# Splitting the first gate-weight load into small pieces on two queues, with the early products reordered to match

## The chip, the cores and the metric

The kernel runs on one core of one Trainium2 chip. The metric is the device time of one execution in microseconds. Executions of the kernel before repeat closely on a quiet chip: three runs gave 179.41 to 180.25 us, median 179.52 us. The traces also give a "span", which is about 1.8 us shorter than the time of the same execution (177.6 us of 179.39 us).

Engines are named as in the profile: PE is TensorE (matrix products), PEld its weight loads, ACT is ScalarE, DVE is VectorE, POOL is GpSimd, SP is SyncE (it issues most DMAs). PSUM is the memory that PE writes its products to, and from which ACT and DVE copy them. In the traces here each engine works through its own instructions in the order in which the program lists them, ready or not.

## The reference, cut to what matters

```python
def reference(A_x, A_w_r, A_w_i, B_x, B_w_gate, B_w_up, B_w_down):
    x = A_x                                       # 1 x 2048 x 512, bf16
    xn = _layernorm(x, axis=-1)
    # A: rfft2 of xn, times (w_r + i w_i), irfft2
    # B: (gelu(xn @ w_gate) * (xn @ w_up)) @ w_down,   512 -> 1792 -> 512
    return x + _A_ref(xn, A_w_r, A_w_i) + _B_ref(xn, B_w_gate, B_w_up, B_w_down)
```

Everything starts from xn, and the first products of B need three things: a normalised and transposed tile of x (128 rows), the gate weights, and the up weights.

## The kernel before

The 2048 rows are 16 tiles of 128. A weight "slice" is 128 columns of the 1792; `e` runs over the four blocks of 128 along the inner dimension of 512. The kernel does not write its instructions in a fixed order. It lists operations with assumed durations, dependencies and priorities, and a small scheduler (`_Plan`), which runs when the kernel is built, simulates them and fixes each engine's order from that. What the planner believes about a DMA's landing is this:

```python
if o.nbytes:                                   # a DMA
    wire = max(wire, o.end + 1.0) + o.nbytes / 0.34e6
    o.end = wire + 1.0                         # its landing, as the plan sees it
```

The loads of the opening, in order of issue:

```python
load_x(0, 1)                                   # x tile 0, 128 KB
d_ident = load_ct("ident", "ident", "ACT")
load_x(1, 1)
load_w(0, 2, ("SP", "ACT"))                    # gate and up slices 0-1, 256 KB each
# ... activation table load on ACT ...
load_x(2, 2)                                   # x tiles 2-3, 256 KB
load_w(2, 4)
load_w(4, 6)
load_x(4, 4)
load_w(6, 10)
load_x(8, 4)
load_w(10, 14)
```

Layernorm of the first four tiles, on DVE but for one small step on POOL, and the transposes. Tile 0 is handled in two halves, which share one PSUM tile:

```python
def pe_transpose(c, due):
    b = _Buf("S")
    n = len(XN[c])
    for h in range(n):
        # ...
        def mm(h=h, es=es):
            if h == 0:
                psum(f"tp.{c}", [P, NE, P], BF16)          # one tile for both halves
            for e in es:
                nc.tensor.transpose(tiles[f"tp.{c}"][:, e], xn[:, c, e * P:(e + 1) * P], ident)

        def ev(es=es, eng=(nc.scalar.copy, V.tensor_copy)[h]):   # half 0 copied by ACT, half 1 by DVE
            eng(out=xnT[c // 4][:, es[0]:es[-1] + 1, c % 4], in_=tiles[f"tp.{c}"][:, es[0]:es[-1] + 1])
        # ...

first = layernorm(0, 1, -28, (), 2)
layernorm(1, 1, -25, first)
for c in range(4):
    if c == 2:
        layernorm(2, 2, -22, XT[0])
    pe_transpose(c, -28 + 3 * c)
    if c < NGAP:
        dummies(GAP, -29.9 + 3 * c, XN[c], P)              # dummy products
```

The first products (`glu(first tile, tiles, first slice, slices)`), two slices at a time, gate then up:

```python
FIRST = [(0, 1, 0, 4), (1, 1, 0, 4), (0, 2, 4, 2), (2, 2, 0, 2), (2, 2, 2, 2), (2, 2, 4, 2)]
```

Of the kernel before, what the change touches and what calls it, by code (L numbers as in the profile page):

```python
# [10 lines left out]
P = 128  # L11
# [6 lines left out]
S = 2048  # L18
D = 512
# [109 lines left out]
class _Plan:  # L129
# [19 lines left out]
    def run(self):  # L149
# [11 lines left out]
        while left:  # L161
            nxt, moved = None, False
            for e, ops in waiting.items():
# [6 lines left out]
                for o in ops:  # L170
                    if any(d.end is None for d in o.deps):
                        continue
                    at = max([d.end + d.lag + self.HOP for d in o.deps if d.eng != "PE" or o.eng != "PE"] + [0.0])
                    if o.nbytes and o.eng != "POOL" and len(lanes) >= 8:
                        at = max(at, sorted(lanes)[-8])
                    if at > now + 1e-9:
                        nxt = at if nxt is None else min(nxt, at)
                        continue
                    held = [rings[b.tag][-self.bufs[b.tag]] for b in o.new if len(rings[b.tag]) >= self.bufs[b.tag]]
                    if any(b.free is None for b in held):  # L180
                        continue
                    at = max([b.free for b in held] + [0.0])
                    if at > now + 1e-9:
                        nxt = at if nxt is None else min(nxt, at)
                        continue
                    if best is None or (o.prio, o.n) < (best.prio, best.n):
                        best = o
# [31 lines left out]
def kernel(  # L219
# [44 lines left out]
    warm = pc.tile([P, D], BF16, name="warm")  # L264
    eps = pc.tile([P, 2], F32, name="eps")
    tiles = {}

# [45 lines left out]
    def load_x(c0, n, eng="SP", deps=()):  # L313
        q = nc.sync if eng == "SP" else nc.scalar
        o = load(n * P * D * 2, lambda: q.dma_start(out=x_t[:, c0:c0 + n], in_=x_v[:, c0:c0 + n]), deps, eng=eng)
        for c in range(c0, c0 + n):
            XD[c] = o

    def load_w(f0, f1, engs=("SP", "SP")):
        a, b = f0 * P, f1 * P  # L320
        os = []
        for t, v, e in ((Wg_sb, wg_v, engs[0]), (Wu_sb, wu_v, engs[1])):
            q = nc.sync if e == "SP" else nc.scalar
            os.append(load(NE * P * P * 2 * (f1 - f0),
                           lambda t=t, v=v, q=q: q.dma_start(out=t[:, :, a:b], in_=v[:, :, a:b]), eng=e))
        for f in range(f0, f1):
            WD[f] = os

    def load_ct(first, last, eng="SP", deps=(), **kw):
        a, b = ccols[first][0], sum(ccols[last])  # L330
        q = nc.sync if eng == "SP" else nc.scalar
        return load(P * 2 * (b - a), lambda: q.dma_start(out=CT[:, a:b], in_=cap[:, a:b]), deps, eng=eng, **kw)

    load_x(0, 1)
    d_ident = load_ct("ident", "ident", "ACT")
    load_x(1, 1)
    load_w(0, 2, ("SP", "ACT"))
    add("ACT", 1.3, lambda: nc.scalar.activation(out=eps[:, 1:2], in_=eps[:, 0:1], func=AF.Gelu_apprx_tanh),
        (o_eps,), -900)
    load_x(2, 2)  # L340
    load_w(2, 4)
    load_w(4, 6)
    load_x(4, 4)
    load_w(6, 10)
    load_x(8, 4)
    load_w(10, 14)

# [26 lines left out]
    wb = _Buf("S")  # L374
    NWARM, NGAP, GAP = 10, 1, 4

# [21 lines left out]
    def layernorm(c0, n, due, after=(), halves=1):  # L398
        k = slice(c0, c0 + n)
        ag = []  # L400
        for c in range(c0, c0 + n):
            s = dve(0.6, lambda c=c: stats(c), [XD[c]] + list(after), due - 3.0 + 0.01 * (c - c0))
            ag.append(dve(0.15, lambda c=c: V.bn_aggr(out=mv[:, c], in_=tiles["st", c][:]), (s,), due - 3.2, ))
        e = dve(0.07, lambda: V.tensor_scalar(  # L404
            out=ve[:, k], in0=mv[:, k, 1], scalar1=EPS, scalar2=None, op0=ALU.add), ag, due - 5)
        r = add("POOL", 0.55, lambda: nc.gpsimd.tensor_tensor(  # L406
            out=rstd[:, k], in0=ve[:, k], in1=half[:, k], op=ALU.pow), (e, o_mem[1]), due - 5, lag=0.1)
        for c in range(c0, c0 + n):
            XN[c] = []
            for h in range(halves):  # L410
                d = slice(h * D // halves, (h + 1) * D // halves)
                XN[c].append(dve(0.04 + 0.29 / halves, lambda c=c, d=d: V.tensor_scalar(  # L412
                    out=xn[:, c, d], in0=x_t[:, c, d], scalar1=mv[:, c, 0:1], scalar2=rstd[:, c:c + 1],
                    op0=ALU.subtract, op1=ALU.mult), (r,), due - 2.5))
        return ag

    def pe_transpose(c, due):
        XT[c] = []
        b = _Buf("S")
        n = len(XN[c])  # L420
        for h in range(n):
            es = range(h * NE // n, (h + 1) * NE // n)

            def mm(h=h, es=es):
                if h == 0:
                    psum(f"tp.{c}", [P, NE, P], BF16)
                for e in es:
                    nc.tensor.transpose(tiles[f"tp.{c}"][:, e], xn[:, c, e * P:(e + 1) * P], ident)

            def ev(es=es, eng=(nc.scalar.copy, V.tensor_copy)[h]):  # L430
                eng(out=xnT[c // 4][:, es[0]:es[-1] + 1, c % 4], in_=tiles[f"tp.{c}"][:, es[0]:es[-1] + 1])

            o = pe(0.24 / n, mm, (XN[c][h], d_ident), due - 2, new=(b,) if h == 0 else (), use=(b,))
            XT[c].append((act, dve)[h](0.1 + 0.35 / n, ev, (o,), due - 30, use=(b,)))
# [4 lines left out]

    first = layernorm(0, 1, -28, (), 2)  # L440
    layernorm(1, 1, -25, first)
    for c in range(4):
        if c == 2:
            layernorm(2, 2, -22, XT[0])
        pe_transpose(c, -28 + 3 * c)
        if c < NGAP:
            dummies(GAP, -29.9 + 3 * c, XN[c], P)
    for c0, n, due in ((4, 2, 14), (6, 2, 16), (8, 4, 24), (12, 4, 32)):
        layernorm(c0, n, due)
        for c in range(c0, c0 + n):  # L450
# [10 lines left out]
    for k in range(2):  # L461
        for c, s, a, n in ((2, 1, 0, 7 * KC), (0, 0, 0, KC), (1, 1, 7 * KC, KC)):
            d_tw.append(dma(P * n * 2, lambda k=k, c=c, s=s, a=a, n=n: gather(k, s, c, a, n),
                            [g_idx] + XN[11], 20, eng="POOL", issue=1.2))

# [20 lines left out]
    def glu(c0, n, f0, nf=1, extra=()):  # L486
# [10 lines left out]
        def mm(nm, W, tag, a, b):  # L497
            if a == 0:
                psum(f"{nm}.{key}", [P, D], tag=tag)
            for f in range(a, b):  # L500
                for e in range(NE):
                    nc.tensor.matmul(tiles[f"{nm}.{key}"][:, f * w:f * w + w], lhsT=W[:, e, (f0 + f) * P:(f0 + f + 1) * P],  # L502
                                     rhs=rhs(e), start=(f + e == 0), stop=(f == nf - 1 and e == NE - 1),
                                     skip_group_check=nf > 1)

        g = [o for c in range(c0, c0 + n) for o in XT[c]]
        step = min(nf, 2)
        us = []
        for a in range(0, nf, step):
            deps = g[-1:] if a else g  # L510
            new = [([], []), ([gb], [ub])][a == 0]
            g = [pe(step * dur, lambda a=a: mm("g_ps", Wg_sb, "G", a, a + step), deps + [WD[f0 + a][0]], t,
                    new=new[0], use=(gb,))]
            us = [pe(step * dur, lambda a=a: mm("u_ps", Wu_sb, "U", a, a + step), us + g + [WD[f0 + a][1]], t,
                     new=new[1], use=(ub,))]
# [20 lines left out]

    FIRST = [(0, 1, 0, 4), (1, 1, 0, 4), (0, 2, 4, 2), (2, 2, 0, 2), (2, 2, 2, 2), (2, 2, 4, 2)]
    for c, n, f, nf in FIRST + [(0, 4, f, 1) for f in range(6, NFC)]:
        glu(c, n, f, nf)
# [387 lines left out]
```

## Time and profile before

| | before |
|---|---|
| median of three executions | 179.52 us |
| span of the profiled one | 177.6 us |
| PE busy | 173.4 us, 98% of the span |
| first PE instruction | 1.34 us |
| PE products and transposes | 1,100 |

The first lines are from the page of the kernel before: its span, the busy time of each engine, PE's busy tenths in 40 slices of the span, and the chain of work that ended last, by engine and by line (only the engine line is kept).

```profile
span 177.6 us, 3041 instructions
...
PE 173.4 (98%) x1100; PEld 92.9 (52%) x1100; DVE 118.1 (66%) x266; ACT 87.4 (49%) x158; POOL 18.6 (10%) x33
...
PE   6999999999999999999999999999999999999993
...
PE 91%; ACT 3%; DVE 3%; issue 1%; POOL 0%; DVEq 0%; POOLq 0%
```

PE is full from end to end, so a change can win only where PE is not full: the first slices. To see how much that is, take the start times of the single PE instructions. Back to back, products start every 56 ns for 128 columns, 109 ns for 256 and 216 ns for 512. What a start-to-start step takes beyond that is *excess*. The span is then the first PE start (1.34 us) + the ideal time of all products (169.73 us) + excess (3.62 us) + the tail from the last PE start to the end (2.92 us) = 177.6 us. Of the 3.62 us, 2.28 lie before 5.6 us (mostly ten dummy products of 512 columns, of which most start every 427 ns instead of 216; the texts call that pace cold), 1.06 between 5.6 and 12.3 us, none up to 60 us, and 0.28 is one stall at 75.7 us.

This is the table of stretches of the kernel before. Its columns are start and end of the stretch and its length, then busy time and (instructions) of each engine, the granted clock, the DMA engines' busy share, and the GB/s they moved.

```profile
0.00:5.60 5.60, 4.26 (x10) 1.31 (x10) 1.99 (x6) 1.49 (x2) 2.11 (x9) 1.00 0.62 182
5.60:12.30 6.70, 6.66 (x93) 5.82 (x92) 4.10 (x14) 2.84 (x6) 1.27 (x2) 1.00 1.08 330
12.30:60.00 47.70, 47.70 (x317) 27.12 (x315) 40.89 (x91) 29.81 (x56) 15.21 (x22) 1.00 0.79 209
```

This is the timeline of the opening of the kernel before. The columns are start, duration, engine, line, operation, out<-in, and in brackets how long the engine was idle before and what released it.

```profile
5.78 0.65 PE L428 MATMUL tp<-CT,xn 128*128 128x128 bf16 x4
...
6.47 0.37 ACT L431 COPY xnT<-tp 128x256 bf16<-128x256 bf16 x1 [3.29 <-PE tp L428]
...
6.88 0.29 DVE L431 COPY xnT<-tp 128x256 bf16<-128x256 bf16 x1 [0.83 <-ACT xnT L431]
6.89 0.82 PE L502 MATMUL g_ps<-xnT,Wg_sb 128*128 128x128 bf16 x8
...
8.42 0.59 ACT L431 COPY xnT<-tp 128x512 bf16<-128x512 bf16 x1 [1.58 <-PE tp L428]
...
8.84 0.62 PE L502 MATMUL u_ps<-xnT,Wu_sb 128*128 128x128 bf16 x8
```

Read it so: ACT copies the first transposed half of tile 0 at 6.47. DVE's copy of the other half waits for ACT's, and PE's first real product starts at 6.89. Tile 1 is copied by ACT at 8.42 and is therefore ready at 9.01.

### The profile page before, as it was taken

Reading aid. Unit: us, or ns where it says so; the run is one execution under the profiler, and the core shown is the slowest. Engines: PE = TensorE matmul, PEld = TensorE weight load, DVE = VectorE, ACT = ScalarE, POOL = GpSimd, SP = SyncE. Lnnn points to the kernel's source line nnn. Section 1 sums busy time; section 2 is a strip of 40 time slices with the busy share of each in tenths; the row PEclk is TensorE's granted clock in tenths of the full one; section 3 lists DMA queues with packets and bytes.
Section 4 is the critical chain, followed back from the end, with each engine's and each line's share of the span. In section 5 each row is a group of like instructions: output and inputs, shape, how many; then the busy total and the mean of one; then the engine's idle time right before and its main releaser. Section 6 shows DMA issues by size and latency. Waiting matters only on the chain.

```text
span 177.6 us, 3041 instructions
## 1 busy us (share of the span) xinstructions
PE 173.4 (98%) x1100; PEld 92.9 (52%) x1100; DVE 118.1 (66%) x266; ACT 87.4 (49%) x158; POOL 18.6 (10%) x33
## 2 busy tenths in 40 slices
PE   6999999999999999999999999999999999999993
PEld 2598545545554544554555455554445444544463
DVE  1869999999537995889999885336442541632522
ACT  3162437456789737999998855453111211211100
POOL 3212138743200000000000000000000000000000
PEclk9999999999999999999999999999999999999999
DMA  5999487999297001302211121100222221322212
GB/s 144 311 355 359 86 270 84 223 296 193 52 347 255 2 0 29 93 2 59 61 48 37 37 59 37 27 0 0 84 68 66 83 89 59 92 80 69 74 45 59
DMA packets 23182, 19.24 MB, mean 108 GB/s; under 512 B 8512, under 2 KB 21824, under 8 KB 23168
## 3 DMA queue, kind: packets, MB, share of 16 engines
q1 hardware_dynamic: 22176, 17.57, 35.0%
q0 software_dynamic: 320, 1.19, 3.1%
q10 hardware_dynamic: 672, 0.30, 0.6%
q8 instruction: 8, 0.13, 0.3%
q14 instruction: 6, 0.05, 0.1%
HBM read 13.28 MB, written 2.10 MB: 87 GB/s over the span
## 4 chain that ended last, share of the span: by engine, by line
PE 91%; ACT 3%; DVE 3%; issue 1%; POOL 0%; DVEq 0%; POOLq 0%
PE u_ps L502 25%; PE g_ps L502 25%; PE warm L380 3%; ACT E L652 2%; PE yp L818 2%; PE bp L581 2%; PE gp L767 2%; PE yp__2078 L872 2%; PE yp__1994 L872 2%; PE yp__1967 L872 2%; PE yp__1936 L872 2%; PE yp__1909 L872 2%; PE yp__1820 L872 2%; PE yp__1793 L872 2%; PE yp__1762 L872 2%; PE yp__1735 L872 2%
## 5 line engine op out<-in xcount | busy, mean ns | idle before, releaser
L502 PE MATMUL g_ps<-xnT,Wg_sb 128*128 128x512 bf16 (+2 forms) x264 | 58.1, 347 | 0.0
L502 PE MATMUL u_ps<-xnT,Wu_sb 128*128 128x512 bf16 (+2 forms) x264 | 57.9, 347 | 0.0
L527 DVE TENSOR_TENSOR hT<-u_ps,ge 128x512 bf16<-128x512 f32 x56 | 38.4, 685 | 17.5 <-PE u_ps L502 14.4
L519 ACT ACTIVATE ge<-g_ps 128x512 bf16<-128x512 f32 x56 | 33.5, 598 | 30.5 <-PE g_ps L502 26.5
L502 PEld LDWEIGHTS <-Wu_sb 128*128 128x128 bf16 x264 | 24.3, 98 | 22.3 <-DMA Wu_sb<-in_B_w_up_dram 0.2
L502 PEld LDWEIGHTS <-Wg_sb 128*128 128x128 bf16 x264 | 24.3, 98 | 20.7 <-issue 0.2
L872 PEld LDWEIGHTS <-hT 128*128 128x128 bf16 x252 | 23.0, 98 | 21.9
L824 ACT CAST yf<-yp 128x512 bf16<-128x512 f32 x16 | 9.3, 586 | 37.6 <-PE yp L818 37.6
L652 ACT CAST E<-ep 64x512 bf16<-64x512 f32 x32 | 18.5, 579 | 1.1 <-PE ep L646 0.7
L396 DVE BATCH_NORM_STATS2 st<-x_t 128x6 f32<-128x512 bf16 x16 | 10.5, 676 | 4.8 <-DMA x_t<-in_A_x_dram 4.8
L629 ACT CAST ds<-dp 128x512 bf16<-128x512 f32 x16 | 8.8, 589 | 1.1 <-PE dp L624 1.0
L773 ACT CAST Gs<-gp 128x512 bf16<-128x512 f32 x16 | 8.6, 593 | 1.0 <-PE gp L767 1.0
L406 POOL TENSOR_TENSOR rstd<-ve,half 128x2 f32<-128x2 f32 (+2 forms) x7 | 6.6, 949 | 21.9 <-DVE ve L404 21.9
L585 ACT CAST Bs<-bp 128x512 bf16<-128x512 f32 x16 | 8.3, 603 | 0.5 <-PE bp L581 0.5
L818 PEld LDWEIGHTS <-Gs 128*128 128x128 bf16 x64 | 4.8, 98 | 3.5
L380 PE MATMUL warm<-warm 128*128 128x512 bf16 (+1 forms) x14 | 5.1, 539 | 1.3 <-POOL half L373 1.3
L412 DVE TENSOR_SCALAR xn<-x_t,mv,rstd 128x512 bf16<-128x512 bf16 (+1 forms) x17 | 6.1, 399 | 0.3 <-POOL rstd L406 0.3
L818 PE MATMUL yp<-CT,Gs 128*128 128x128 bf16 x64 | 6.0, 219 | 0.0
L683 DVE TENSOR_TENSOR m<-X,TW 128x1024 bf16<-128x1024 bf16 x8 | 5.5, 692 | 0.2
L624 PEld LDWEIGHTS <-Bs 128*128 128x128 bf16 x64 | 4.4, 98 | 2.4
L689 DVE TENSOR_TENSOR m<-X,TW 128x1024 bf16<-128x1024 bf16 x8 | 5.5, 684 | 0.0
L646 PE MATMUL ep<-ds,CT 128*128 128x512 bf16 x16 | 5.4, 379 | 0.0
(103 smaller groups left out, 169.0 us busy)
## 6 DMA issues: line engine op xcount, KB each, us to landing
y<-in_A_x_dram SPq DMA_DIRECT2D x16, 128.0 KB, 2.1
F<-F SPq DMA_DIRECT2D x32, 64.0 KB, 2.0
out_dram<-y SPq DMA_DIRECT2D x15, 128.0 KB, 1.7
Wd_sb<-in_B_w_down_dram SPq DMA_DIRECT2D x2, 896.0 KB, 8.3
x_t<-in_A_x_dram SPq DMA_DIRECT2D x3, 512.0 KB, 6.8
Wg_sb<-in_B_w_gate_dram SPq DMA_DIRECT2D x2, 512.0 KB, 6.8
Wu_sb<-in_B_w_up_dram SPq DMA_DIRECT2D x2, 512.0 KB, 9.1
Wg_sb<-in_B_w_gate_dram SPq DMA_DIRECT2D x3, 256.0 KB, 5.1
```

The lines of the kernel that those rows point to most:

```text
L380: nc.tensor.matmul(tiles["warm"][:, 0:w], lhsT=warm[:, 0:P], rhs=warm[:, 0:w], start=True, stop=True)
L396: V.bn_stats(out=st[:], in_=x_t[:, c])
L502: nc.tensor.matmul(tiles[f"{nm}.{key}"][:, f * w:f * w + w], lhsT=W[:, e, (f0 + f) * P:(f0 + f + 1) * P], rhs=rhs(e), start=(f + e == 0), ...
L519: nc.scalar.activation(out=e[:, 0:nf * w], in_=tiles[f"g_ps.{key}"][:, 0:nf * w], func=AF.Gelu_apprx_tanh)
L527: V.tensor_tensor(out=out, in0=tiles[f"u_ps.{key}"][:, 0:nf * w].rearrange("p (f w) -> p f w", w=w) if nf > 1 else tiles[f"u_ps.{key}"][:, ...
L585: nc.scalar.copy(out=o, in_=tiles[f"bp.{cg}.{q}"][:].rearrange("p c (r g a) -> p (c r) g a", r=2, a=4))
L629: nc.scalar.copy(out=ds[:].rearrange("p (s k t) -> p s k t", s=2, t=2), in_=tiles[f"dp.{G}"][:].rearrange("p s t k -> p s k t"))
L652: nc.scalar.copy(out=tiles[f"E.{g}"][64 * h:64 * h + 64, r], in_=tiles[f"ep.{g}.{h}"][64 * r:64 * r + 64])
L773: nc.scalar.copy(out=o, in_=tiles[f"gp.{g}.{h}"][:].rearrange("p q (n a) -> p (q n) a", a=4))
L818: nc.tensor.matmul(yp[:, q], lhsT=tiles["G"][:, q, c], rhs=IQ[q], start=(q == 0), stop=(q == 3), skip_group_check=True)
L824: nc.scalar.copy(out=tiles[f"yf.{c // 2}"][:, c % 2], in_=tiles[f"yp.{c}"][:])
L872: nc.tensor.matmul(y[:, s], lhsT=tiles[sb, f][:, cl * P:(cl + 1) * P], rhs=Wd_sb[:, f, s], start=(f == 0), stop=False)
```

## The change

The intent: let the first gate products start as early as they can, by loading gate slices 0–3 as four 128 KB pieces (one per block `e`) on two queues, with products in the order in which the pieces arrive (first those of blocks 0 and 1, then those of 2 and 3); and let PE have tile 1 early, by normalising tiles 1 and 3 on ACT. The diff, cut to its core:

```diff
-    load_w(0, 2, ("SP", "ACT"))
+    d_g = [load_first(e, eng) for e, eng in ((1, "ACT"), (0, "SP"), (3, "ACT"), (2, "SP"))]   # gate slices 0-3, 4 x 128 KB
     # ... activation table load on ACT ...
+    d_u = load(NE * P * P * 8, lambda: nc.sync.dma_start(out=Wu_sb[:, :, 0:4 * P], in_=wu_v[:, :, 0:4 * P]))  # up 0-3, 512 KB
     load_x(2, 2)
-    load_w(2, 4)
-    load_w(4, 6)
+    load_w(4, 8)
     load_x(4, 4)
-    load_w(6, 10)
+    load_w(8, 11)
     load_x(8, 4)
-    load_w(10, 14)
+    load_w(11, 14)
@@ planner: it assumes 1 (x tiles 0, 1), 1.9 (later x tiles) or 2 to 2.3 bytes (weights) an element, before 2
@@ (the true size) for all, and a dependency on the same engine costs no hop any more
-    NWARM, NGAP, GAP = 10, 1, 4
+    NWARM, NGAP, GAP = 10, 1, 2
@@ new: layernorm_act(c, ...): two passes on ACT (Identity with accumulated sum, Square with accumulated sum)
@@ transposes: each half its own PSUM tile
-                if h == 0:
-                    psum(f"tp.{c}", [P, NE, P], BF16)
+                psum(f"tp.{c}.{h}", [P, NE, P], BF16)
-    first = layernorm(0, 1, -28, (), 2)
-    layernorm(1, 1, -25, first)
-    for c in range(4): ...
+    layernorm(0, 1, -28, (), 2)
+    layernorm_act(1, -25, 2)
+    pe_transpose(0, -28)
+    dummies(GAP, -29.9, XN[0], P)
+    pe_transpose(1, -25)
+    layernorm(2, 1, -22, XN[1])
+    pe_transpose(2, -22)
+    layernorm_act(3, -19, 1, XT[0], XT[1])
+    pe_transpose(3, -19)
-        layernorm(c0, n, due)
+        layernorm(c0, n, due, XN[3])              # tiles 4-15 only after tile 3
@@ the table gathers on POOL may start early
-                            [g_idx] + XN[11], 20, eng="POOL", issue=1.2))
+                            [g_idx] + XN[3], 20, eng="POOL", issue=1.2))
@@ products
-            for f in range(a, b):
-                for e in range(NE):
+            for f, e in sorted(((f, e) for f in range(a, b) for e in range(NE)), key=lambda k: (k[1] // 2, k)):
-        step = min(nf, 2)
+        step = 4 if n == 1 else min(nf, 2)
-    FIRST = [(0, 1, 0, 4), (1, 1, 0, 4), (0, 2, 4, 2), (2, 2, 0, 2), (2, 2, 2, 2), (2, 2, 4, 2)]
+    FIRST = [(0, 1, 0, 4), (1, 1, 0, 4), (0, 2, 4, 2), (2, 1, 0, 4), (3, 1, 0, 4), (0, 2, 6, 2), (2, 2, 4, 2), (2, 2, 6, 2)]
```

## The prediction

> **What bounds the kernel now.** TensorE. The page gives PE 173.4 us busy of a 177.6 us span. By the single instructions' start times, back-to-back products start every 56 ns (128 columns), 109 ns (256) and 216 ns (512). That agrees with the Trainium skill, "TensorE: Matmul & The Clock Gate", section "Wait — 56ns, not 53.3ns?" (columns / 2.4 GHz + about 2.5 ns; cold 107 ns for 128 columns, as the dummies here show). Over the 1,100 PE instructions only 3.6 us of start-to-start time exceeds that rule: 2.1 us is ten cold 512-column dummies, 0.28 us one stall at 75.7 us, and nearly all the rest lies before 8.9 us. So the change can only win in the opening, and win little.
>
> **The opening now (timeline).** First x tile lands 3.48; statistics 3.51, rstd on GpSimd 4.76, xn 5.38; transposes 5.78; ScalarE copy 6.47 to 6.84; VectorE's copy of the other half 6.88 to 7.17, which waits for ScalarE's. First real product 6.89. Stalls after it: 0.21 us (7.0, second transposed half) and 0.17 us (8.67, up weights of slices 2–3, landed 8.80). Then PE is gapless. At 11.53 it has done 64 products and 12 transposes since 6.89: 4.25 us of work in 4.64 us.
>
> **What the change does.**
> 1. The transpose's halves get separate PSUM tiles. The Trainium skill, "PSUM — Partial Sum Buffer", section "Terms", says two engines may not use one bank at once; the wait between the copies looks kept for that. Estimate: ScalarE's copy 6.2 to 6.6, VectorE's 6.5 to 6.8; first product near 6.6 (−0.3 us), partly at the cold clock (+0.1). The 0.21 us stall goes (−0.2).
> 2. Gate slices 0–3 come as four 128 KB pieces on both queues. That makes 800 KB, where 800 KB of today landed by 5.85 us, so they don't limit: the layernorm chain does. Up slices 0–3 (512 KB) come next: at today's 250 to 340 KB/us they land at 7.1 to 7.8. Gate products of tile 0 end near 7.5: new wait 0 to 0.4 us.
> 3. x tiles 2–3 land near 8.2 instead of 6.73; their products move after tiles 0–1's slices 4–5, whose weights land near 9.6 and 11. Stall 0 to 0.3 us.
> 4. Tiles 1 and 3 are normalised on ScalarE (two passes of about 0.65 us), which is idle 3.2 to 6.5. Tile 1 is ready about 1 us earlier; this fills PE, and is not itself critical. I expect no second table load.
> 5. More narrow products: 32 of 256 columns become 64 of 128 (+0.08 us), 16 of 512 become 32 of 256 (+0.04 us).
> 6. The order elsewhere is re-planned, and the table gathers may start 15 us earlier, beside the weights. PE stays full; ±0.3 us.
>
> **Sum.** −0.3 −0.2 +0.1 (opening), +0.2 (up weights), +0.1 (tiles 2–3), +0.12 (narrow products), −0.1 (chance at the later stall): about −0.1, at best −0.5 us. With the best case weighed in I predict 179.2 us against 179.52, range 178.5 to 180.0. Chances: faster by over 2% 0.01, within 2% 0.98, slower by over 2% 0.01.
>
> **What would show the steps right.** Timeline: VectorE's copy starts without waiting for ScalarE's; first gate product at 6.5 to 6.7; one table load; a PE wait for the up weights after the first 16 gate products, under 0.4 us; gapless PE from about 11 us; PE busy within 0.5 us of 173.4.
>
> **What would make it wrong.** The first x tile or the up weights land later than the byte count says; tiles 2–3 reach PE's queue before their data, stalling it by 1 us; a PE gap long enough to return the clock to half speed; a second table load (1.28 us each here); new stalls in the filter stage near 60 to 76 us.

## The result, and the profile after

The changed kernel took 180.89 us (median of six runs, 180.47 to 181.38); the kernel before took 179.50 us on the same chip (179.39 to 180.25). The ratio is 1.0073, with a 95% interval of 1.0051 to 1.0096. Ratios here are the mean time of one kernel's fast runs over that of the other's in the same rounds, so not quite the ratio of the medians. That is within 2%, but it is slower, by 1.4 us, and outside the predicted range of 178.5 to 180.0 us.

These are the same page lines of the kernel after.

```profile
span 179.0 us, 3142 instructions
...
PE 172.4 (96%) x1146; PEld 94.5 (53%) x1146; DVE 118.3 (66%) x265; ACT 90.1 (50%) x166; POOL 16.8 (9%) x34
...
PE   6779999999999999999999999999999999999993
...
PE 92%; DMA 4%; SPq 1%; ACT 1%; issue 0%; DVE 0%
```

Two things are new: the 2nd and 3rd slices of PE's row fell from 9 to 7, and the chain of work that ended last has a DMA in it for 4% of the span. The table of stretches of the kernel after, with columns as above, says where:

```profile
0.00:5.60 5.60, 4.26 (x12) 1.55 (x13) 1.63 (x5) 3.02 (x6) 2.13 (x9) 1.00 0.63 177
5.60:12.30 6.70, 4.60 (x77) 4.21 (x75) 3.25 (x11) 3.10 (x9) 1.34 (x3) 1.00 1.02 349
12.30:60.00 47.70, 47.70 (x373) 29.50 (x371) 41.38 (x90) 29.37 (x54) 13.33 (x23) 1.00 0.82 207
```

Between 5.6 and 12.3 us PE was busy 4.60 us of 6.70, against 6.66 before. The DMA engines were not slower in it: 349 GB/s against 330. The view of the waits of PE in the kernel after (engine, what it waited for, us in total, times, longest) names them; the 1.3 us before the warm-up products is the same in both kernels, and is the only entry in the kernel before.

```profile
PE g_ps L524 <- ACT xnT L453: 1.4, 2, 1.2
PE warm L388 <- POOL half L381: 1.3, 1, 1.3
PE u_ps L524 <- DMA Wu_sb<-in_B_w_up_dram: 0.7, 1, 0.7
```

The timeline of the opening of the kernel after, with columns as before:

```profile
5.80 0.37 ACT L453 COPY xnT<-tp 128x256 bf16<-128x256 bf16 x1 [0.20 <-PE tp L450]
...
5.91 0.29 DVE L453 COPY xnT<-tp 128x256 bf16<-128x256 bf16 x1
6.22 1.05 PE L524 MATMUL g_ps<-xnT,Wg_sb 128*128 128x128 bf16 x16 [0.24 <-ACT xnT L453]
...
7.11 0.39 PE L450 MATMUL tp<-CT,xn 128*128 128x128 bf16 x4
...
8.18 1.07 PE L524 MATMUL u_ps<-xnT,Wu_sb 128*128 128x128 bf16 x16 [0.68 <-DMA Wu_sb<-in_B_w_up_dram]
...
9.40 0.63 ACT L420 ACTIVATE xn<-x_t 128x512 bf16<-128x512 bf16 x1 [3.23 <-DMA x_t<-in_A_x_dram]
9.40 0.69 DVE L404 BATCH_NORM_STATS2 st<-x_t 128x6 f32<-128x512 bf16 x1 [2.33 <-DMA x_t<-in_A_x_dram]
...
10.01 0.27 DVE L453 COPY xnT<-tp 128x256 bf16<-128x256 bf16 x1
10.03 0.35 ACT L453 COPY xnT<-tp 128x256 bf16<-128x256 bf16 x1
...
10.43 0.38 PE L524 MATMUL g_ps<-xnT,Wg_sb 128*128 128x128 bf16 x4 [1.19 <-ACT xnT L453]
```

The reader should see three things. First, the start is what the change wanted: DVE's copy no longer waits for ACT's (5.91 against 5.80), and the first product starts at 6.22 instead of 6.89. Second, the gate products of tile 0 are done near 7.1, and PE waits for the up weights, which landed at 8.13. By start times that stall is 0.84 us (the bracket says 0.68, because it counts from the modelled end of the product before). Third, the transposes of tile 1 were made at 7.11 to 7.5, but their two copies ran only at 10.01 and 10.03. In ACT's order the statistics pass of tile 3 stands ahead of the copy, and in DVE's order the statistics of tile 2 stand ahead of theirs. Both wait for x tiles 2–3, landed at 9.38. ACT stood idle for 3.23 us and DVE for 2.33 us, and for the last 1.9 us of that, from 7.5 us on, the copy behind was ready. PE's gate products of tile 1 therefore started at 10.43; by start times the stall is 1.35 us. Products that needed nothing but tile 1 and weights that had long landed waited for the data of tiles 2 and 3.

The chain of work that ended last, in order of time, tells it in one piece (start, length, what) for the kernel after:

```profile
3.07 6.31 DMA x_t<-in_A_x_dram
9.38 0.02 issue
9.40 0.72 ACT xn L420 x2
10.12 0.27 ACT xnT L453
10.39 0.04 issue
10.43 1.05 PE g_ps L524 x16
```

Landings of the opening, from the single DMA records (us):

| | before | after |
|---|---|---|
| x tile 0 / x tile 1 | 3.48 / 3.84 | 3.03 / 4.01 |
| gate, first | slices 0–1: 5.85 | pieces of 0–3: 4.19, 5.76, 5.94, 6.57 |
| up, first | slices 0–1: 5.30; 2–3: 8.80 | slices 0–3: 8.13 |
| x tiles 2–3 | 6.73 | 9.38 |
| next gate / next up | slices 4–5: 9.65 / 10.45 | slices 4–7: 10.90 / 12.38 |

Ahead of x tiles 2–3 the changed kernel issues 1,312 KB of loads (gate and up slices 0–3 among them), the kernel before 800 KB.

The sum of the difference, by start times (us):

| part of the span | before | after | difference |
|---|---|---|---|
| first PE start | 1.34 | 1.34 | 0 |
| products at their own pace | 169.73 | 169.74 | +0.01 |
| excess before 5.6 us | 2.28 | 1.99 | −0.29 |
| excess 5.6 to 12.3 us | 1.06 | 2.59 | +1.53 |
| excess 12.3 to 60 us | 0 | 0 | 0 |
| excess after 60 us (stall at 75.7) | 0.28 | 0 | −0.28 |
| tail: last PE start to end | 2.92 | 3.35 | +0.43 |
| span | 177.6 | 179.0 | +1.40 |

The +1.53 us are the two new stalls (0.84 and 1.35), less the two of 0.21 and 0.17 us that are gone, less 0.28 us ahead of the first product. The −0.29 us before 5.6 us may be chance: this term was 1.99 to 2.52 us in the ten traces with the changed loads and ACT normalising, and 2.11 to 2.76 us in five of the kernel before and its near variants (before, p1, e8, e11, t2).

The tail was a surprise. At the end SyncE checks the completion semaphores of the DMAs one after the other, always in the same order. These are its check-off steps in the two kernels, in us after the last product's start, each with the semaphore it checks:

```
before: S100 1.01  S101 1.07  S110 1.13  S111 1.19  S113 1.25  S115 1.31  S117 1.37  S118 2.03   end 2.92
after:  S100 2.03  S101 2.09  S110 2.16  S111 2.22  S113 2.28  S114 2.34  S116 2.40  S117 2.46   end 3.35
```

The last output's DMA is the one that finishes at about 2.03. Before, it signals S118, the last in the row, so the other seven were ticked off while it was under way. After, it signals S100, the first, so seven more steps of about 0.06 us follow it: 7 × 0.06 = 0.43 us. The eight semaphores are handed out in rotation, and the changed kernel has one DMA more.

### The profile page after: what moved, and what is told of

Same layout as the page of the kernel before. It is cut to its first block, busy times and chain, and to the rows that moved or that the text cites. A ratio compares the mean times of both kernels' runs of the same rounds, so it can differ in the third digit from the quotient of the medians.

```text
span 179.0 us, 3142 instructions
## 1 busy us (share of the span) xinstructions
PE 172.4 (96%) x1146; PEld 94.5 (53%) x1146; DVE 118.3 (66%) x265; ACT 90.1 (50%) x166; POOL 16.8 (9%) x34
## 3 DMA queue, kind: packets, MB, share of 16 engines
q0 software_dynamic: 320, 1.19, 3.0%
## 4 chain that ended last, share of the span: by engine, by line
PE 92%; DMA 4%; SPq 1%; ACT 1%; issue 0%; DVE 0%
PE g_ps L524 27%; PE u_ps L524 27%; DMA x_t<-in_A_x_dram 4%; PE yp L840 2%; PE gp L789 2%; PE dp L646 2%; PE bp L603 2%; PE ep L668 2%; PE yp__2130 L894 2%; PE yp__2077 L894 2%; PE yp__2046 L894 2%; PE yp__2019 L894 2%; PE yp__1988 L894 2%; PE yp__1961 L894 2%; PE yp__1872 L894 2%; PE yp__1845 L894 2%
## 5 line engine op out<-in xcount | busy, mean ns | idle before, releaser
L524 PEld LDWEIGHTS <-Wu_sb 128*128 128x128 bf16 x288 | 25.4, 98 | 22.7 <-DMA Wu_sb<-in_B_w_up_dram 0.8
L524 PEld LDWEIGHTS <-Wg_sb 128*128 128x128 bf16 x288 | 25.0, 98 | 21.1 <-issue 1.6
L404 DVE BATCH_NORM_STATS2 st<-x_t 128x6 f32<-128x512 bf16 x14 | 9.4, 673 | 5.4 <-DMA x_t<-in_A_x_dram 5.4
L430 POOL TENSOR_TENSOR rstd<-ve,half 128x1 f32<-128x1 f32 (+2 forms) x8 | 6.1, 763 | 24.0 <-DVE ve L412 22.2
L436 DVE TENSOR_SCALAR xn<-x_t,mv,rstd 128x512 bf16<-128x512 bf16 (+1 forms) x15 | 5.5, 396 | 0.8 <-POOL rstd L430 0.8
L388 PE MATMUL warm<-warm 128*128 128x512 bf16 (+1 forms) x12 | 4.6, 551 | 1.3 <-POOL half L381 1.3
L789 PEld LDWEIGHTS <-F 128*128 128x128 bf16 x64 | 4.2, 98 | 1.9
```

Of the source, the lines that this page charges most:

```text
L404: V.bn_stats(out=st[:], in_=x_t[:, c])
L524: nc.tensor.matmul(tiles[f"{nm}.{key}"][:, f * w:f * w + w], lhsT=W[:, e, (f0 + f) * P:(f0 + f + 1) * P], rhs=rhs(e), start=(f + e == 0), ...
```

## The experiments

**Theories.** A: two waits in the opening cost the time, the up weights' landing and the copies of tile 1 that are queued behind work for tiles 2–3. B (rival): the gathers on POOL, which the change lets start at 12.8 us instead of 27.4, get in the way of the other engines. C: the tail depends only on which semaphore the last DMA gets, so on the number of DMAs. The expectations below use these letters or spell the rival out.

All runs gave correct results. Each was timed in five rounds beside the kernel before on the same chip. The table gives first the times (median of the fast runs: six of each kernel unless marked, seven of e11; the kernel before has 11 runs per chip), then what its profiled run shows by start times: excess up to 12.3 us, excess from 12.3 to 60 us, and tail.

| run (chip) | us, median (range) | ratio, 95% interval | to 12.3 | 12.3–60 | tail |
|---|---|---|---|---|---|
| before / after (first chip) | 179.50 / 180.89 | 1.0073 [1.0051, 1.0096] | 3.34 / 4.58 | 0 / 0 | 2.92 / 3.35 |
| e1_copies_first (7) | 181.11 (180.75–182.83) † | 1.0048 [0.9987, 1.0108] | 3.77 | 2.84 | 3.36 |
| e2_up_in_four (7) | 182.63 (182.42–182.96) | 1.0136 [1.0098, 1.0174] | 3.99 | 2.52 | 3.16 |
| e6_true_landings (7) | 182.37 (181.43–183.25) | 1.0116 [1.0072, 1.016] | 3.23 | 3.04 | 3.36 |
| e8_before_new_rule (7) | 179.81 (179.40–180.09) | 0.9971 [0.9933, 1.0009] | 3.69 | 0.56 | 2.92 |
| c1_changed_again (5) | 181.22 (180.59–182.92) | 1.0045 [0.9992, 1.0099] | 4.23 | 0.13 | 3.36 |
| e5_gathers_late (5) | 181.72 (180.19–182.62) | 1.0044 [0.9983, 1.0105] | 4.47 | 0.79 | 3.35 |
| e10_copies_first_gathers_late (5) | 181.86 (181.51–182.04) | 1.0055 [1.001, 1.0099] | 4.04 | 1.76 | 3.35 |
| e11_before_gathers_early (5) | 180.71 (180.60–182.16) | 0.9996 [0.9952, 1.004] | 3.34 | 2.76 | 2.92 |
| t1_changed_one_dma_fewer (8) | 181.52 (180.99–182.21) | 1.0057 [1.0011, 1.0102] | 4.79 | * | 2.92 |
| t2_before_one_dma_more (8) | 180.47 (180.32–180.61) | 1.0001 [0.996, 1.0042] | 3.51 | * | 3.37 |
| b1_true_landings_late_gathers (8) | 180.71 (180.40–182.90) | 1.0038 [0.9981, 1.0094] | 2.89 | * | 2.92 |
| b2_smaller_pieces (8) | 181.28 (180.86–182.92) † | 1.0074 [1.0015, 1.0132] | 2.84 | * | 2.92 |
| p1_before_own_tiles (15) | 179.85 (179.30–180.30) | 0.9967 [0.9928, 1.0006] | 3.40 | 0.80 | 2.92 |
| p2_before_new_loads (15) | 183.11 (182.46–183.97) | 1.0147 [1.01, 1.0195] | 3.95 | 3.49 | 3.36 |
| p3_before_new_loads_own_tiles (15) | 182.71 (182.15–183.65) | 1.0127 [1.0084, 1.017] | 3.95 | 3.20 | 3.36 |
| p4_all_but_new_loads (15) | 181.38 (180.78–181.80) | 1.0050 [1.0008, 1.0091] | 3.24 | 2.79 | 2.92 |

† Some executions fall into a slower state and are left out: three of e1's seven (183.89 to 184.36 us) and one of b2's six (184.27).

\* In these four traces 17 or 18 product records are missing, spread over the time from about 19 us on, which inflates the excess there; the column is not used. The column "to 12.3" also moves by up to 0.8 us with the landing of x tile 0, for which PE waits before 5.6 us: that part of it was 1.99 to 2.76 us in all runs.

The kernel before had medians of 180.14, 181.29, 180.00 and 179.88 us on chips 7, 5, 8 and 15. Its own runs there spread by 2.0 to 2.4 us (two slow ones, 204.7 us on chip 5 and 308 us on chip 8, are left out), much more than on the first chip. So on these chips totals do not resolve differences of a few tenths. The changed kernel itself was timed again only on chip 5 (c1), so on chips 7, 8 and 15 the runs compare with the kernel before alone. **The verdicts on the parts rest on the single stalls that the profiles show before 12.3 us and on the tail**, and totals are used only where the interval is clear of 1.

### Theory A: the order behind which tile 1's copies stand

**e1_copies_first.** The work for tiles 2 and 3 may come only after the copies of tile 1.

```diff
-    layernorm(2, 1, -22, XN[1])
+    layernorm(2, 1, -22, XT[1])
-    layernorm_act(3, -19, 1, XT[0], XT[1])
+    layernorm_act(3, -19, 1, XT[1], XT[1])
```

> The changed kernel, with one thing altered: the statistics of x tiles 2 and 3 may be queued on VectorE and ScalarE only after both copies of tile 1's transpose (before: after earlier work). Theory (the two in-order queues stand at a wait for x tiles 2-3, landed 9.38, with tile 1's copies behind it): the copies end near 8 instead of 10.4, the 1.35 us PE stall before tile 1's gate products is gone; PE then meets the up weights of slices 4-7 (landed 12.38) about 0.6 us early, so the total falls by 0.8 to 1.2 us, to 179.7 to 180.1. Rival (the time is lost elsewhere: longer ScalarE work, narrow products, the re-planned later stages): within 0.3 us of the changed kernel's 180.9.

The timeline of PE in this run:

```profile
7.16 0.54 PE L450 MATMUL tp<-CT,xn 128*128 128x128 bf16 x4
8.60 1.07 PE L524 MATMUL u_ps<-xnT,Wu_sb 128*128 128x128 bf16 x16 [0.90 <-DMA Wu_sb<-in_B_w_up_dram]
9.50 1.06 PE L524 MATMUL g_ps<-xnT,Wg_sb 128*128 128x128 bf16 x16
```

The gate products of tile 1 follow the up products of tile 0 without a gap. The stall of 1.35 us is gone, though no load was touched: its cause was the order of the copies, not the bandwidth. The wait for the up weights stays (1.06 us by start times; they landed 0.4 us later here). The up products of slices 4–5 end at 13.16 us instead of 14.19, so 1.0 of the 1.35 us was kept to that point. The total did not show it: in the profiled execution a new stall of 2.48 us appears at 19.7 us, of which more below. That execution (182.83 us) is the slowest of the four fast ones; the others took 180.75 to 181.29 us. On the total the expectation (179.7 to 180.1) was missed.

**e6_true_landings.** No instruction and no DMA is altered, only what the planner believes, and so the order that it fixes: the gate pieces and x tiles 2–3 count for more bytes, so that their planned landings come near the measured ones. In the changed kernel's own plan x tiles 2–3 land at 7.71 us (measured 9.38), the up weights at 6.98 (8.13), the last gate piece at 5.43 (6.57).

```diff
-    return load(P * P * 8, ...out=Wg_sb[:, e, 0:4 * P]...
+    return load(P * P * 8 * 1.7, ...out=Wg_sb[:, e, 0:4 * P]...
-        o = load(n * P * D * (1.9 if c0 > 1 else 1), ...
+        o = load(n * P * D * (3.2 if c0 == 2 else 1.9 if c0 > 1 else 1), ...
```

> The changed kernel with no DMA altered: only the byte counts that the schedule's planner assumes for the four gate pieces (x1.7) and for x tiles 2-3 (1.9 to 3.2 per element) are raised, so that its planned landings (gate 6.5, up 8.1, x tiles 2-3 9.3) agree with the trace. Theory (the order was frozen for landings 1.6 us too early): tile 1's copies come before the statistics of tiles 2-3 in both queues, the 1.35 us stall is gone, total 179.6 to 180.1 as in the run with the copies first. Rival: no change (180.6 to 181.1).

The timeline of PE in this run:

```profile
6.88 1.17 PE L524 MATMUL g_ps<-xnT,Wg_sb 128*128 128x128 bf16 x16
7.88 0.39 PE L450 MATMUL tp<-CT,xn 128*128 128x128 bf16 x4
8.18 1.07 PE L524 MATMUL u_ps<-xnT,Wu_sb 128*128 128x128 bf16 x16
9.08 1.06 PE L524 MATMUL g_ps<-xnT,Wg_sb 128*128 128x128 bf16 x16
9.97 1.06 PE L524 MATMUL u_ps<-xnT,Wu_sb 128*128 128x128 bf16 x16
```

Both stalls are gone; the excess between 5.6 and 12.3 us is 0.71 us, against 2.59. The first product came later here (6.88; x tile 0 landed at 3.73), so that the up weights were no longer waited for is luck; only the stall at tile 1 is the repair's. That supports theory A: the order had been frozen on landings 1.1 to 1.7 us too early. Again the total (1.0116) did not follow: 2.0 us of stalls between 16.9 and 19.5 us.

**e2_up_in_four.** The up slices 0–3 are loaded as four pieces too.

```diff
-    d_u = load(NE * P * P * 8, ... Wu_sb[:, :, 0:4 * P] ...)
+    d_u = [load(P * P * 8, lambda e=e: ... Wu_sb[:, e, 0:4 * P] ...) for e in range(NE)]
```

> The changed kernel, with the up slices 0-3 loaded as four 128 KB pieces instead of one of 512 KB. Theory: the first up products start at 7.4 to 7.7 instead of 8.18, so the 0.84 us PE stall shrinks by 0.3 to 0.7 us; but the next stall ends at a fixed time (x tiles 2-3 landing at 9.4, then ScalarE's pass and copy to 10.4), so it grows by as much and the total stays within 0.25 us of the changed kernel's 180.9. Rival (the two stalls add up independently): 0.3 to 0.7 us faster than the changed kernel.

From its timeline of PE:

```profile
7.49 1.32 PE L525 MATMUL u_ps<-xnT,Wu_sb 128*128 128x128 bf16 x16
8.64 1.06 PE L525 MATMUL g_ps<-xnT,Wg_sb 128*128 128x128 bf16 x16
...
11.61 1.05 PE L525 MATMUL g_ps<-xnT,Wg_sb 128*128 128x256 bf16 x8 [1.01 <-DMA Wg_sb<-in_B_w_gate_dram]
```

The wait for the up weights shrank from 0.84 to 0.25 us, because the first pieces are usable before the last: the first up products started at 7.49, as expected. The rest was missed. The new plan also put tile 1's copies ahead of the statistics of tiles 2 and 3, so that stall is absent here (gate products of tile 1 from 8.64), and the run is no test of the up load alone. PE then stopped for slices 4–7, until 11.61 us: the stall there is 1.18 us. Much of what is won at one landing is lost at the next. The total (1.0136) is well above what was expected; 2.52 us of excess lie after 12.3 us. The tail was 3.16 us: three DMAs more move the last one from S100 to S111, three places further down the row of checks, 3 × 0.06 us less.

**c1_changed_again.** The changed kernel as it is, on another chip, as a control.

> The changed kernel unaltered, as the control on this chip: the chip of the last four runs showed before itself at 180.1 and more spread than the first one (179.5). Both theories: 1 to 2 us slower than before on the same chip. If the stalls of semaphore updates seen at 17 to 21 us in three of the last runs belong to the early table gathers, some executions of this one show them too.

The two stalls are there again: the wait for the up weights 0.70 us, for tile 1's copies 1.00 us, and the tail is 3.36. They are no accident of the first trace. The total is not clear here: 181.22 us against 181.29 for the kernel before on this chip, and an interval that includes 1, so the expected loss of 1 to 2 us was not shown again.

### One part of the change at a time

**p2_before_new_loads.** The kernel before with the new loads, product order and byte counts alone; tiles 1 and 3 stay on DVE.

```diff
-    load_w(0, 2, ("SP", "ACT"))
+    d_g = [...four pieces...]; d_u = load(...up slices 0-3...); load_w(4, 8); load_w(8, 11); load_w(11, 14)
-            for f in range(a, b): for e in range(NE):
+            for f, e in sorted(..., key=lambda k: (k[1] // 2, k)):
-        step = min(nf, 2)
+        step = 4 if n == 1 else min(nf, 2)
```

> The kernel before, with the new loads alone (gate slices 0 to 3 as four pieces on two queues, up slices 0 to 3 as one load, the later weights in the new sizes, products ordered by pairs to match, the planner's byte counts that go with them). Tiles 1 and 3 stay on VectorE, the first list and the gathers stay as before. Theory A (the loads bring two waits: up weights at 8.1 us, tiles 2 and 3 at 9.4 us): first product near 6.4 (the first x tile lands near 3.0), a stall of 0.5 to 1.0 us that ends when the up weights land (8.0 to 8.3), and the x tiles 2 and 3 near 9.4 with a second stall of 0.5 to 2 us before 11.6, because VectorE has the statistics of tiles 2 and 3 ahead of work that PE needs, or because slices 4 and 5 land at 10.9 and 12.4. Excess before 12.3 us 4 to 5.5 instead of 3.34. Theory C: three loads more become one DMA more than before, so the tail is 3.3 to 3.4 instead of 2.92. Ratio 1.006 to 1.012. Rival (it was ScalarE's normalising that hurt, not the loads): excess 3.0 to 3.5, ratio about 1.002.

Its timeline of PE (not its whole opening):

```profile
6.81 1.05 PE L507 MATMUL g_ps<-xnT,Wg_sb 128*128 128x128 bf16 x16 [0.24 <-ACT xnT L437]
...
11.68 1.05 PE L507 MATMUL g_ps<-xnT,Wg_sb 128*128 128x256 bf16 x8 [0.71 <-DMA Wg_sb<-in_B_w_gate_dram]
13.65 0.34 PE L434 MATMUL tp<-CT,xn 128*128 128x128 bf16 x3 [0.92 <-DVE xn L418]
```

This is the slowest of all, 1.0147, more than I had expected. The stall I expected for the up weights did not come, because the first product came later (6.81; x tile 0 landed at 3.52 here). Instead PE waits for gate slices 4–7 (0.87 us) and, at 12.5 us, 1.08 us for tile 2, whose statistics started at 10.18 when x tiles 2–3 had landed. Up to 27 us the excess is 5.26 us, against 3.34 before. So the loads by themselves bring about 1.9 us of waits; the ACT passes are not needed for that. Which wait it becomes depends on the order. Not separated by any run: how much of it comes from the split of the gate load, and how much from the 512 KB more that stand ahead of x tiles 2–3. The tail rose to 3.36 as expected. (2.18 us of excess between 27 and 60 us come on top; see below.)

**p4_all_but_new_loads.** The mirror image: the changed kernel with loads, product order, first list and gathers put back. Separate PSUM tiles, ACT normalising, two dummies and the planner's rule stay.

> The changed kernel with the loads, the products' order and the first list put back as before, and the gathers late as before. What stays of the change: separate PSUM tiles, tiles 1 and 3 normalised on ScalarE, fewer dummies, the planner's rule. Theory A (the loads and what waits on them cost the time): x tiles 2 and 3 land near 6.7 again, before ScalarE's pass of tile 3 is in the way, so no stall above 0.4 us in the opening, excess before 12.3 us 2.7 to 3.3, tail 2.92, and a time equal to or up to 0.4 us below the kernel before (ratio 0.997 to 1.001). This is the candidate to beat both. Rival (ScalarE's passes ahead of the copies hurt wherever tiles 2 and 3 land): a stall near 1 us before tile 1's gate products remains, ratio 1.004 or more.

Its timeline of ACT:

```profile
6.73 0.63 ACT L414 ACTIVATE xn<-x_t 128x512 bf16<-128x512 bf16 x1 [0.16 <-DMA x_t<-in_A_x_dram]
7.27 0.19 ACT L414 ACTIVATION_READ_ACCUMULATOR xn<-x_t 128x1 f32 x1
7.54 0.37 ACT L447 COPY xnT<-tp 128x256 bf16<-128x256 bf16 x1
```

The same queue order (statistics of tile 3 ahead of the copy of tile 1) costs ACT 0.16 us of idle time here instead of 3.23, because x tiles 2–3 land near 6.7 again. From the first product on no stall before 12.3 us is over 0.15 us, and the excess to there is 3.24. So the order alone was harmless with the old loads, and the loads alone (p2) cost about 2 us. The expectation for the opening held. That for the total did not (1.0050 instead of at most 1.001): 2.56 us of excess lie between 27 and 60 us.

**p1_before_own_tiles.** The kernel before with separate PSUM tiles for the two transposed halves and nothing else. All DMA, PE, SP and POOL orders in the plan are unchanged.

> The kernel before, with one part of the change alone: each half of tile 0's transposes gets its own PSUM tile. No DMA and no TensorE, VectorE or GpSimd order is touched. If the wait between the two copies is kept only because they share a PSUM tile (step 1 of the prediction), the VectorE copy starts within 0.15 us of the ScalarE copy, the 0.21 us stall after the first two pairs of products (at 6.95 us in the profile before) is gone, the first product stays at 6.8 to 6.9 us, and the opening's excess before 12.3 us falls from 3.34 to about 3.1. In time that is -0.2 us, ratio 0.998 to 1.000. If the two copies wait for something else, nothing changes. Tail 2.92.

In its timeline the copies of ACT and DVE overlap. ACT first:

```profile
5.94 0.37 ACT L430 COPY xnT<-tp 128x256 bf16<-128x256 bf16 x1 [2.75 <-PE tp L427]
```

and DVE:

```profile
6.20 0.29 DVE L430 COPY xnT<-tp 128x256 bf16<-128x256 bf16 x1 [0.32 <-PE tp L427]
```

DVE now waits for its own transposes (done at 6.19), not for ACT's copy, and the 0.21 us stall at 7.0 is gone. So that wait came from the shared tile. ACT's copy gains too: it starts when the first two transposes are done (5.90), and in the kernel before only when all four are (6.43). The first product started at 6.36, earlier than the 6.8 to 6.9 that I expected. Yet the excess to 12.3 us is 3.40 (expected 3.1) against 3.34 before: PE then waits 0.46 us for gate slices 2–3 (to 8.00) and 0.45 us for up slices 2–3 (to 8.91). The time was 179.85 against 179.88 us. An earlier first product was worth nothing here, where the second pair of slices is what PE waits for next.

**p3_before_new_loads_own_tiles.** Both parts, p1 and p2, together (diff as in those).

> The two parts together: the new loads and the separate PSUM tiles. Theory A: the first product 0.3 to 0.5 us earlier than in the run with the new loads alone, or the same with the 0.21 us stall gone, but the waits for the up weights and for tiles 2 and 3 grow by what is won, so the time is the same as with the new loads alone within 0.2 us. Rival: the gains add up, and it is 0.3 us faster than the new loads alone.

The excess to 12.3 us is 3.95, as in p2, and 1.3 from there to 27 us, as in p2. The rival (gains add up) would have needed 0.3 us less. The medians, 182.71 and 183.11, lie within each other's ranges.

**e8_before_new_rule.** The kernel before with the planner's new rule for dependencies on the same engine.

> The kernel before with only the planner's new timing rule (an operation may follow one on its own engine without the assumed hop). Theory (the loss is in the opening's loads and queue order, not in the re-planned rest): within 0.2 us of before, 179.3 to 179.7. Rival (the re-planned later stages cost time): 0.3 us or more slower than before.

It is as fast as before (0.9971, interval up to 1.0009). The re-planned rest of the kernel does not cost anything. The stall of 0.28 us near 75.7 us is absent here, as in every other run with the new rule, and stands (0.27 or 0.28 us) in every run with the old one: so the new rule's order took it away in the changed kernel.

### Theory C: the tail

**t1_changed_one_dma_fewer** loads the down weights with one DMA instead of two; **t2_before_one_dma_more** cuts one of the two in the kernel before.

```diff
  t1 (on the changed kernel)
-    two loads: Wd_sb[:, 0:7], Wd_sb[:, 7:14]
+    one load:  Wd_sb[:, 0:14]
  t2 (on the kernel before)
-    two loads: Wd_sb[:, 0:7], Wd_sb[:, 7:14]
+    three:     Wd_sb[:, 0:7], Wd_sb[:, 7:11], Wd_sb[:, 11:14]
```

> The changed kernel with the two loads of the down weights issued as one transfer; the order of TensorE, ScalarE and VectorE is the same, one DMA less in all. Theory C (the program's end: SyncE steps through the eight DMA semaphores in a fixed order, about 0.06 us each, and the last output's DMA sits on the first of them in the changed kernel, on the last of them in before, because the changed kernel issues one DMA more): from TensorE's last start to the end 2.92 us instead of 3.35, total 0.43 us below the changed kernel (about 0.5 us below 180.9 to 181.2). Rival (the longer end comes from the output's transfer itself): 3.35 us stays.

> The kernel before with the second load of the down weights cut in two, orders otherwise the same. Theory C: the end grows from 2.92 to 3.35 us, total +0.43 us over before. Rival: 2.92 us stays, total equal to before within 0.15 us.

The last DMA moved to the last semaphore in the first (S117, checked at 2.03 us) and to the first in the second (S100, checked at 2.05 us, seven more to go). The tails are 2.92 and 3.37 us. This is shown in both directions, and p2, p3 and e2 fit it. In these runs one DMA more or less moved the tail by up to 0.45 us. The totals on this chip are too spread to show it: t2's ratio is 1.0001, with an interval that includes both no change and +0.43 us.

### Theory B: the gathers

**e5_gathers_late** and **e10_copies_first_gathers_late** put the gathers of the changed kernel (and of e1) back to where they were; **e11_before_gathers_early** gives the kernel before the early gathers.

```diff
  e5, e10
-                            [g_idx] + XN[3], 20, eng="POOL", issue=1.2))
+                            [g_idx] + XN[11], 20, eng="POOL", issue=1.2))
  e11: the reverse, on the kernel before
```

> The changed kernel with one thing altered: the six table gathers wait for x tile 11's normalisation (as before, about 27 us) instead of tile 3's (12 us). TensorE's and ScalarE's orders are the same as in the changed kernel. Theory A (only the two waits at 7.3 and 9.0 us cost): within 0.2 us of the changed kernel on this chip. Theory B (early gathers beside the weight loads delay semaphore updates and instruction supply at 13 to 22 us): 0.4 to 2 us faster than it, with less spread, and the profile has no PE gap over 0.3 us between 12 and 27 us.

> The run with tile 1's copies queued first, plus the gathers late. TensorE's and ScalarE's orders as in that run (182.8 median, 180.8 to 184.4). Theory A+B: the 1.35 us stall of the opening is gone and no stall takes its place at 17 to 21 us: 0.8 to 1.3 us faster than the changed kernel with late gathers, and within 0.5 us of before on this chip. If theory B is wrong, the stall at 17 to 21 us stays and the median is over 182.

> The kernel before with one thing altered: the table gathers wait for x tile 3's normalisation (about 11 us) instead of tile 11's. TensorE's and ScalarE's orders are those of before. Theory B: slower than before by 0.5 to 3 us in at least some executions, with delayed semaphore updates at 12 to 22 us in the trace. Theory A: within 0.2 us of before.

Undoing the early gathers leaves the opening as it was (4.47 us of excess to 12.3 us in e5, 4.04 in e10) and moves the later stalls: none from 12.3 to 27 us any more, 0.79 and 1.76 us from 27 to 60 us. The totals gained nothing: e5 took 181.72 us against 181.22 for the changed kernel on this chip (c1), and e10, with the repair of e1, 181.86, where 0.8 to 1.3 us less than e5 had been expected. In e11 PE stands for 2.76 us at 13.2 us, with gathers issued from 9.7 to 20.7 us; that is the slowest of its executions (182.16 us), the six others took 180.60 to 180.81, and the ratio is 0.9996. In e1, e6 and e11 the records show PE's and ACT's semaphore updates arriving late: products in e1 that ended at 18.2, 19.1 and 20.0 us were reported at 21.5 to 21.6 us. In all traces in which I saw such late reports they lie between the start of the gathers and a few us after their end, early or late (in p2 and p4 between 27 and 36 us). The two traces of the first chip have no such report, with early gathers (12.8 to 20.9 us) and with late ones. So theory B does not explain the 1.4 us of the first chip. It does go with what blurred the totals on the other chips; whether and how the gathers, or the chip, delay the reports is left open.

### Looking for a better version

**b1_true_landings_late_gathers** joins e6, e5 and t1; **b2_smaller_pieces** adds up weights and slices 4–7 in smaller loads and the down weights in four.

```diff
  b2, on top of b1
-    load_w(4, 8)
+    load_w(4, 6)
+    load_w(6, 8)
  and d_u as in e2, the down weights as four loads
```

> The changed kernel with three mends: planned landings as measured (PE stall of 7 to 12 us was 0.7 us in that run, against 2.6), gathers late, one DMA fewer. Theories A and C: PE excess between 5.6 and 12.3 us 0.6 to 1.0, end 2.92 us, total 0.3 to 0.8 us below before where the chip is quiet; delays at the gathers (27 to 36 us) may take it back. If A is wrong: slower than before.

> As the last one, plus the up slices 0-3 in four pieces and the weights of slices 4-7 in two loads each (down weights in four so that the end stays 2.92 us). Theory A: up products of tile 0 start by 7.6, the products of slices 4-5 don't wait for 6-7; PE excess between 5.6 and 12.3 us 0.4 to 0.9; total within 0.3 us of the last one, below before. Rival (small pieces cost bandwidth: landings later): PE excess over 1.2.

Both have the best openings, 2.89 and 2.84 us of excess against 3.34 in the kernel before, and the short tail. b1 took 180.71 us against 180.00 (an interval that includes 1), and b2 was slower, 181.28 us; neither was below the kernel before, as I had expected them to be. In b1 three stalls of 0.78, 0.48 and 0.67 us stand at 37.8, 39.2 and 44.4 us, in the 9 us after its gathers (28.6 to 35.5 us). No version was shown to beat the kernel before. At most 0.5 us could be had from the opening, and the disturbance later in the program is larger than that.

## Why the prediction was wrong

The class (within 2%) was right; the time was not, and the sign was not: −0.3 us predicted, +1.4 measured. Point by point, as the prediction numbered them:

1. *Separate PSUM tiles, first product near 6.6 (−0.3, −0.2, +0.1).* Right, and larger: 6.22. DVE's copy started 0.11 us after ACT's. The surplus is luck: x tile 0 landed 0.45 us earlier, and the transposes started every 55 to 57 ns, where in the trace of before they and the dummies after them started every 79 to 107 ns where nothing held them up. Both paces occur with the same kernel (the changed one had the slow pace in e5's trace, whose orders are the same up to there). From the first transpose to the first product it took 0.73 us (p1: 0.75) against 1.11 (e11 and t2, at the fast pace: 1.00), so about 0.25 us are the tiles' and 0.1 us the pace's. p1 shows that the cause was right, and also that the saving is worth nothing by itself.
2. *Up weights at 7.1 to 7.8, wait 0 to 0.4 us (counted +0.2).* Wrong size. They landed at 8.13, and the wait was 0.84. The error is in "at today's 250 to 340 KB/us they land at": I gave the bytes issued up to that load the whole bandwidth. By 7.5 us both kernels had moved about the same (1.64 MB before, 1.60 MB after). The loads up to and including the up weights are 1.34 MB, and when they landed 1.78 MB had been moved: most of the difference belonged to loads issued later, which run at the same time. My first product was also 0.4 us too late, which hid part of the wait.
3. *x tiles 2–3 near 8.2, stall 0 to 0.3 us (counted +0.1).* This is the step that failed most. They landed at 9.38, for the same reason. And the stall (1.35 us) was not in their own products, which I had looked at because they come late in the list, but in those of tile 1. I followed the data dependencies and not the order of the queues: two copies that had everything they needed stood behind statistics that waited for a DMA. The prediction did name "tiles 2–3 reach PE's queue before their data, stalling it by 1 us" as a way to be wrong; it was ACT's and DVE's queues that they reached too early.
4. *Tile 1 about 1 us earlier.* Wrong. Its normalising was early, transposed at 7.5 us, but its copies were done at 10.38, against 9.01 before. "No second table load" was right; there is one, of 1.28 us.
5. *Narrow products +0.12 us.* The sum of all products at their own pace is +0.01 us, 169.74 against 169.73: the two dummies fewer pay for most of the narrow ones.
6. *The rest within ±0.3 us.* Right as to the planned rest: nothing between 12.3 and 60 us, and −0.28 us for the stall at 75.7 us, which vanished. I had given it −0.1 as chance; e8 shows that the planner's rule does it.
7. *Not in the sum at all:* the tail, +0.43 us, from one DMA more. t1 and t2 show it.

Putting measured terms in the place of mine: −0.29 before 5.6 us, +1.53 between 5.6 and 12.3 us, +0.01, −0.28 and +0.43 give +1.40 us. PE busy was said to stay within 0.5 us of 173.4. It fell by 1.0, to 172.4: nearly all the excess of before lay within the modelled durations of the products and counted as busy, while 2.1 us of the excess after are idle time (0.24, 0.68 and 1.19 us in the timeline). "Gapless PE from about 11 us" held.

My rule in the Trainium skill's terms, "TensorE: Matmul & The Clock Gate", section "Wait — 56ns, not 53.3ns?" (columns / 2.4 GHz + about 2.5 ns), held in all traces (56, 109 and 216 ns) and is what made the sums close. What I should have read beside it is "DMA: Bandwidth & Descriptors", section "Issuing engines are not separate DMA queues": transfers from all engines run on the same 16 DMA engines and interleave. The traces fit that: by 6.57 us, when the last of the four pieces landed, the changed kernel had moved 1.32 MB, and the kernel before as much. It is no test of the number of queues, as the kernel before also used both for its first gate and up slices.

What stays open: why semaphore reports come late around the gathers on some chips, so whether e1's or e6's repair would show in the total on a quiet chip. That the repair removes the stalls is shown; that it makes the kernel faster than before is not.

## What to carry to other kernels

When a load order changes, follow every instruction that waits for a load that is now later, on each in-order engine, and ask what ready work stands behind it; a stall shows up at the consumer of *that* work. A schedule frozen on assumed landings is only as good as the landings: compare the planned times with the trace's, and repair the assumption (e6) before the order. And starting the first product earlier was worth nothing here (p1) while the next landing was not earlier too.

## What the Trainium skill lacked or had wrong

- "TensorE: Matmul & The Clock Gate", section "Back-to-back issue gap", gives about 81 ns (128 columns) and 131 ns (512 columns) for a stream of alternating weight loads and products, and calls columns / 2.4 + 2.5 ns the isolated gap. Here such streams start every 56, 109 and 216 ns for 128, 256 and 512 columns; the formula is the one that fits.
- No page that I found describes this part of the program's end: SyncE ticks the DMA completion semaphores off in a fixed order, about 0.06 us each, so the tail after the last product was 2.92, 3.16 or 3.35 to 3.37 us by the place of the last DMA's semaphore alone.
- "DMA: Bandwidth & Descriptors" says that completion is not first-in first-out (section "Queues, rings and completion order"), but gives no size for what that costs a landing. Here x tiles 2–3, with 1.61 MB issued up to and including them, landed when about 2.2 MB had been moved, 9.38 us instead of the 8.2 that the byte count gave.
- "PSUM — Partial Sum Buffer", section "Terms", forbids two engines on one bank at once. The page gives no figure for what that costs a program whose two copies read different halves of one tile: the second copy waited for the first (6.88 against 6.47 us), and with two tiles it started 0.26 us (p1) or 0.11 us (the changed kernel) after it.
- No page that I found mentions that semaphore reports of PE and ACT can come 1 to 5 us late around indirect gathers on POOL; it was seen in traces from four chips (5, 7, 8 and 15), not in those of the first, and its cause is open.
